# Chunk 1's q, k and x turned through DRAM instead of on TensorE, and zero matmuls in the opening, in an mLSTM with a gated FFN

## Chip, cores and metric

One NeuronCore of a Trainium2 chip runs the whole kernel. The metric is the device time of one execution in microseconds. The time before is 537.03 us, the median of three runs (535.66 to 537.51).

## What is computed

An mLSTM recurrence over 768 steps (batch 4, 8 heads, head size 40), and on its output a gated FFN. The reference, cut to what matters:

```
for t in range(S):                                   # S = 768
    m_new = max(f[t] + m, i[t])
    C = exp(f[t]+m-m_new) * C + exp(i[t]-m_new) * outer(v[t], k[t])
    n = exp(f[t]+m-m_new) * n + exp(i[t]-m_new) * k[t]
    y[t] = sigmoid(o[t]) * (C @ q[t]) / max(|n . q[t]|, 1)
x = y as (3072, 320)
out = (sigmoid(x @ w_gate) * (x @ w_val)) @ w_out    # d_ff = 1536
```

The three FFN weights come as 64-bit floats, 3.9 MB each.

## The kernel before

The 768 steps are cut into 6 chunks of 128, and a chunk into 4 units, one for each batch entry: unit n is chunk n // 4, batch entry n % 4. In a chunk the recurrence is attention with a decay matrix: scores k.q (`s`), times the decay (`t`), times v (`av`), plus what the state of earlier chunks gives (`in`), then the state's update (`cs`, `cm`, `ca`). For the scores, q and k must stand with the head's dims on the partitions; they are loaded with time on the partitions, so they must be turned. The same holds for the unit's output x, which the FFN needs turned (`xh`, `xl`: its high part and the rest).

There are three ways of turning, chosen by the chunk (lines 649 to 760). Chunk 0 (`padded`) uses TensorE transposes of zero-padded pairs of heads. Chunk 1 (`not stacked`, lines 726 to 759) makes six TensorE transposes a unit (L736), copies them out of PSUM (L745, L747), spreads q over a block-diagonal matrix by a mask product (`qb`, L752), and makes the scores of a group of heads with one fp32 matmul of 384 or 256 columns (L759; an fp32 matmul is two instructions in the trace). Its x is turned by three more transposes (L948), after a copy (`xd`, L942). Chunks 2 to 5 (`bounced`, lines 649 to 697) turn 32 x 32 blocks on VectorE (`tq`, L656), write them to a DRAM buffer `scq` with four DMAs (`tw`, L647), read q and k back stacked by six DMAs (`sr`, L668) and once more plainly for the state product (`sq`, L688, L690), form high and low parts with a sign vector on ScalarE and VectorE (`sh`, `sl`, L674, L680), and make the scores of a head with one fp32r matmul of 128 columns (L697). Their x goes the same way through `scx` (`tx`, `xw`, `xr`, L926 to L938). The stacked tiles `bh` and `bl`, the tile `kh` of the block transposes and the tile of the turned x have one buffer each; `scq` and `scx` have two, taken in turn by the batch entry.

The FFN of a chunk goes over 12 slices of d_ff. A step `n` makes two products of gate and value (`u0`, `u1` with the rests `r0`, `r1`: L1025, L1029, L1030), their activation and product (`th`, `gx`, `gh`, `gl`), and the down projection (`dn`, L1062 to L1064). In chunk 0 the weights are split into high and low parts as they come in (`wd` loads, `wa` to `wl` work on them).

All instructions are issued in the order of one list written out in the kernel, `ORDER` (lines 42 ff.); an engine runs its own in that order. Nearly every DMA is issued on SP's queue, in list order; only the input gates and q of unit 0 go on ScalarE's. Every element of the list is a function `@op(name)`. The first FFN step stands behind the attention of units 0 to 2. In the opening, `wm` (L379) runs eight fp32 matmuls on zeros; the tile of zeros is `warm`, of which `tab` (L309) overwrites one element to load the activation table.

What switches the ways, in `PARAM`: 'QT': 2 (chunks from 2 on turn q and k through DRAM), 'XT': 2 (the same for x), 'V32': 1.

Of the kernel before, what the change touches and what calls it, by code (L numbers as in the profile page):

```python
# [8 lines left out]
F32 = mybir.dt.float32  # L9
# [13 lines left out]
    'V32': 1,  # L23
    'AV': 2,
    'QT': 2,
    'XT': 2,
# [5 lines left out]
    'PAD': 1,  # L32
    'warm': 8,
    'eng': {
# [8 lines left out]
    i1 li lf i2 wdo0 i0 wz lq0 wdr0 i3 i5 ga tap pz tr0.0 cp0.0 gm0 gb war0 wdv0 tac sp0.0 wao0 wav0 sp1.0 sp1.1 gc  # L43
    wbo0 wco0 sp0.1 gm1 ee0.0 em0.0 wbr0 wcr0 woo0 who0 wor0 lv0 l10 ee1.0 em1.0 wbv0 wcv0 lk0 wlo0 ee0.1 em0.1
    tr0.1 lk1 cp0.1 gs0 lk2 tr1.1 whr0 ee1.1 wlr0 lq1 tr1.0 cp1.0 wdo4 wov0 cp1.1 gm2 whv0 ld2 lq2 wao4 s0.0 wdo1
    wao1 lq4 dl0 t0.1 wbo4 s1.0 kw0 i8 em1.1 dl1 kw1 gs1 lk3 lo0 lq3 tab cs0 cm0.0 wco4 cm0.1 tr2.1 lv1 woo4 who4
    wlv0 l11 tr2.0 t0.0 wdo3 ee2.1 lo1 og0 t1.0 ee2.0 cp2.0 cp2.1 t1.1 av0 wlo4 av1 gm3 wbo1 gm4 tr3.0 ns0 wao3 og1
    cp3.0 nd0 wdg0 ro0 ld3 xd0 xt0 xh0 gm5 ns1 nd1 wco1 wm wdg1 wag0 em2 woo1 who1 ro1 wbg0 xd1 xt1 xh1 wdr1 wbo3
    lv3 wco3 xl0 xl1 s2.0 wcg0 lo2 ee3.1 dl2 kw2 ee3.0 wlo1 em3 gd wag1 wog0 u1.0 lv2 r1.0 l12 t2.0 tbp t2.1 tbc
    whg0 wlg0 og2 wbg1 woo3 wcg1 dl3 cs1 cm1.0 cm1.1 tr3.1 cp3.1 who3 wog1 u0.0 r0.0 kw3 th0 gx0 wlo3 war1 whg1 gh0  # L50
    av2 ns2 u0.1 nd2 gl0 l13 r0.1 s3.0 wbr1 u1.1 dn0.0 wdv1 ld4 r1.1 ee4.1 wcr1 lk4 ee4.0 ro2 wor1 th1 wlg1 t3.0
    wav1 t3.1 tr4.0 gx1 wdo5 wao5 lo4 wbo5 cp4.0 whr1 wbv1 lo3 wcv1 wov1 u0.2 cs2 cm2.0 em4 gs4 wlr1 dn0.1 cm2.1
    wco5 gh1 xd2 ld5 gl1 av3 whv1 nd3 r0.2 dn1.1 og3 ns3 wlv1 xt2 dn1.0 u1.2 r1.2 ee5.0 woo5 th2 xh2 wdo2 i6 tdp xl2
    wao2 wbo2 tdc tr4.2 qb4.0 dl4 ro3 cp4.2 xd3 u0.3 who5 r0.3 gx2 gh2 qb4.2 wco2 gl2 th3 woo2 xt3 xh3 xl3 s4.0 u1.3
# [24 lines left out]
    ee8 em8 gh19 gl19 nd7 dn19.1 s8.0 th20 xh6 u1.20 dn19.0 xl6 r1.20 s8.2 cd7.1 kw7 ro7 dl8 t8.0 kw8 s8.1 gx20
    sr9.00 sr9.02 sr9.10 sr9.12 sr9.01 u0.21 r0.21 t8.2 gh20 th21 cs7 cm7.1 cm7.0 gl20 u1.21 r1.21 gx21 sr9.11 t8.1  # L80
    u0.22 dn20.1 r0.22 in8 ca7.1 gh21 gl21 dn21.1 th22 ti8 u1.22 r1.22 gx22 lk10 l18 dn20.0 gh22 ob0.2 dn21.0 va8
    vb8 u0.23 r0.23 xd7 xt7 gl22 sh9.0 da8 db8 av8.0 sl9.0 xh7 lq11 lv9 th23 av8.1 tq10 tw10.1 av8.2 ad8 u1.23 r1.23
    gx23 ns8 sh9.1 gh23 dn22.1 u0.24 r0.24 gl23 kw9 cd7.0 lv11 dn22.0 tw10.0 sl9.1 dn23.1 xl7 u1.24 r1.24 dn23.0
    tw10.3 ea10 th24 gx24 s9.1 ob0.3 nd8 u0.25 t9.1 r0.25 lq14 tw10.2 gh24 s9.2 gl24 dn24.1 u1.25 og9 r1.25 ee10
    s9.0 sq10.0 t9.2 ro8 t9.0 cs8 sr10.00 sr10.02 th25 gx25 dn24.0 in9 sr10.01 sr10.10 sr10.11 u0.26 da9 r0.26 lk11
    em10 dl10 gh25 gl25 u1.26 r1.26 sr10.12 th26 ca7.0 u0.28 cm8.0 dn25.1 dn25.0 gx26 r0.28 ti9 cm8.1 lq12 kw10 gh26
    cd8.1 gl26 u1.28 r1.28 th28 dn26.1 gx28 gh28 db9 tx8 xw8.3 sh10.0 dn26.0 gl28 sq10.1 u0.27 r0.27 dn28.3 tq11
    tw11.2 tw11.1 th27 xw8.1 tw11.0 l19 dn28.2 u1.27 lq13 r1.27 va9 l111 ca8.1 sh10.1 sl10.0 ld11 gx27 vb9 tw11.3
    u0.29 r0.29 av9.0 av9.1 av9.2 gh27 th29 sl10.1 s10.2 gl27 dn27.1 u1.29 ad9 r1.29 nd9 ns9 dn27.0 gx29 u0.30 r0.30
    t10.2 gh29 xw8.2 s10.0 s10.1 gl29 dn29.3 dn29.2 u1.30 t10.1 ro9 xw8.0 t10.0 th30 lv10 r1.30 in10 cd10.1 gx30  # L90
# [102 lines left out]
def mlstm_then_gated_ffn_kernel(  # L193
# [89 lines left out]
    @op("wz")  # L283
    def _():
        nc.vector.memset(warm, 0.0)

    if PARAM["PAD"]:
        DP = 64
        pads = []
# [826 lines left out]
```

## Time and profile before

| | |
|---|---|
| median of three runs | 537.03 us |
| profiled execution, its own time | 532.81 us |
| span of the profiled execution | 531.1 us |
| mean granted clock of TensorE | 0.986 |
| TensorE busy | 514.0 us (97%) |
| VectorE, ScalarE, GpSimd busy | 333.9, 244.1, 251.9 us |
| moved by DMA | 74.15 MB |

A profile is one execution. PE is TensorE's matmuls, PEld its weight loads, DVE VectorE, ACT ScalarE, POOL GpSimd, SPq the queue on which DMAs are issued. Records of matmuls that follow each other overlap, so their durations hold latency; the distance between starts is what one costs in a row. The DMA share is the mean busy share of 16 DMA engines and can pass 1 where packets overlap. PEclk is the granted clock of TensorE as a share of 2.4 GHz.

### The profile page before, as it was taken

Reading aid. Unit: us, or ns where it says so; the run is one execution under the profiler, and the core shown is the slowest. Engines: PE = TensorE matmul, PEld = TensorE weight load, DVE = VectorE, ACT = ScalarE, POOL = GpSimd, SP = SyncE. Lnnn points to the kernel's source line nnn. Section 1 sums busy time; section 2 is a strip of 40 time slices with the busy share of each in tenths; the row PEclk is TensorE's granted clock in tenths of the full one; section 3 lists DMA queues with packets and bytes.
Section 4 is the critical chain, followed back from the end, with each engine's and each line's share of the span. In section 5 each row is a group of like instructions: output and inputs, shape, how many; then the busy total and the mean of one; then the engine's idle time right before and its main releaser. Section 6 shows DMA issues by size and latency. Waiting matters only on the chain.

```text
span 531.1 us, 10974 instructions
## 1 busy us (share of the span) xinstructions
PE 514.0 (97%) x4005; PEld 474.4 (89%) x4005; DVE 333.9 (63%) x700; ACT 244.1 (46%) x560; POOL 251.9 (47%) x293
## 2 busy tenths in 40 slices
PE   5899999999999999999999999899999999999997
PEld 5789998889999999998888888789888888999996
DVE  6789876877667766665675555957263584643322
ACT  4768757644554353644542353342263334223222
POOL 3746465572474267467485427364513624601000
PEclk9689999999999999999999999999999999999999
DMA  8986868238678988699968699497545846201000
GB/s 190 236 216 185 215 157 225 79 91 174 133 159 162 173 178 189 140 184 179 187 117 157 136 204 158 112 173 178 147 99 94 152 98 134 56 26 42 14 14 25
DMA packets 222477, 74.15 MB, mean 140 GB/s; under 512 B 167380, under 2 KB 214168, under 8 KB 222424
## 3 DMA queue, kind: packets, MB, share of 16 engines
q1 hardware_dynamic: 221336, 73.20, 63.9%
q8 instruction: 31, 0.51, 0.4%
q10 hardware_dynamic: 1088, 0.26, 0.2%
q14 instruction: 22, 0.18, 0.1%
HBM read 61.54 MB, written 11.90 MB: 138 GB/s over the span
## 4 chain that ended last, share of the span: by engine, by line
PE 79%; DMA 7%; SPq 4%; ACT 3%; DVE 3%; issue 2%; POOL 2%; DVEq 0%; POOLq 0%; ACTq 0%
PE pg L1025 33%; PE po L1062 7%; PE po L1064 6%; PE po L1063 6%; PE pg L1029 5%; PE pg L1030 5%; PE av L893 3%; PE av L886 3%; PE s L697 2%; PE cs L969 2%; PE in L869 2%; DMA scx<-tx 2%; DMA qs<-scq 2%; SPq L647 2%; PE s L759 1%
## 5 line engine op out<-in xcount | busy, mean ns | idle before, releaser
L1042 DVE SCALAR_TENSOR_TENSOR pg<-sg,pg 128x256 f32<-128x256 f32 (+1 forms) x103 | 54.8, 532 | 98.1 <-PE pg L1030 72.4
L1047 ACT ACTIVATE gh<-pg 128x256 fp32r<-128x256 f32 (+1 forms) x103 | 48.2, 468 | 139.7 <-DVE pg L1042 122.5
L1025 PE MATMUL pg<-xh,wh 128*128 128x256 f32 (+1 forms) x412 | 105.8, 338 | 0.3 <-ACT xh L955 0.2
L1025 PE MATMUL pg<-xh,wl 128*128 128x256 f32 (+1 forms) x412 | 101.2, 327 | 0.0
L1025 PE MATMUL pg<-xl,wh 128*128 128x256 f32 (+1 forms) x412 | 100.9, 326 | 0.0
L1062 PE MATMUL po<-oh,gh 128*128 128x320 f32 x288 | 94.3, 327 | 0.3 <-ACT gh L1047 0.3
L1064 PE MATMUL po<-oh,gl 128*128 128x320 f32 x288 | 89.4, 310 | 0.2 <-DVE gl L1052 0.2
L1063 PE MATMUL po<-ol,gh 128*128 128x320 f32 x288 | 88.9, 309 | 0.0
L1035 ACT ACTIVATE sg<-pg 128x256 f32<-128x256 f32 (+1 forms) x103 | 48.0, 466 | 66.0 <-PE pg L1030 61.0
L1025 PEld LDWEIGHTS pg<-xl,wh 128*128 128x128 f32 x412 | 69.1, 190 | 7.5 <-POOL xl L959 0.6
L1025 PEld LDWEIGHTS pg<-xh,wl 128*128 128x128 f32 x412 | 69.0, 189 | 7.2
L1052 DVE TENSOR_TENSOR gl<-pg,gh 128x256 fp32r<-128x256 f32 (+1 forms) x103 | 54.1, 526 | 33.0 <-ACT gh L1047 31.7
L1025 PEld LDWEIGHTS pg<-xh,wh 128*128 128x128 f32 x412 | 67.1, 189 | 3.8 <-DVE gl L1052 0.8
L1029 PE MATMUL pg<-xh,w 128*128 128x256 f32 (+1 forms) x206 | 68.3, 331 | 0.0
L1030 PE MATMUL pg<-xl,w 128*128 128x256 f32 (+1 forms) x206 | 67.1, 326 | 0.0
L1062 PEld LDWEIGHTS po<-oh,gh 128*128 128x128 f32 x288 | 54.4, 189 | 3.9 <-ACT gh L1047 0.6
L1063 PEld LDWEIGHTS po<-ol,gh 128*128 128x128 f32 x288 | 54.3, 189 | 3.3
L842 POOL TENSOR_TENSOR dr<-d 128x1024 f32<-128x1024 f32 x16 | 30.3, 1894 | 52.8 <-DVE d L823 50.6
L1064 PEld LDWEIGHTS po<-oh,gl 128*128 128x128 f32 x288 | 54.1, 188 | 1.1 <-DVE gl L1052 1.0
L638 POOL TENSOR_SCALAR_AFFINE_SELECT d<-d 128x1024 f32<-128x1024 f32 x22 | 26.2, 1190 | 41.0 <-ACT d L634 34.9
L823 DVE TENSOR_TENSOR d<-s,d 128x384 f32<-128x384 f32 (+2 forms) x68 | 34.9, 526 | 12.7 <-PE s L697 7.3
L630 POOL TENSOR_TENSOR d<-at,d 128x1024 f32<-128x1024 f32 x16 | 31.3, 1959 | 22.5 <-DMA d<-mscr 18.8
(156 smaller groups left out, 911.3 us busy)
## 6 DMA issues: line engine op xcount, KB each, us to landing
d<-mscr SPq DMA_DIRECT2D x22, 512.0 KB
ks<-scq SPq DMA_DIRECT2D x48, 168.0 KB
qs<-scq SPq DMA_DIRECT2D x48, 168.0 KB
scq<-tq SPq DMA_DIRECT2D x64, 80.0 KB
su_o<-in_moe_w_out_dram SPq DMA_DIRECT2D x12, 320.0 KB
v<-in_v_dram SPq DMA_DIRECT2D x24, 160.0 KB
o<-in_o_gate_dram SPq DMA_DIRECT2D x24, 160.0 KB
out_dram<-ob SPq DMA_DIRECT2D x24, 160.0 KB
```

The source lines that it names most:

```text
L630: E("ea", n).tensor_tensor(dm[n], a, dm[n], ALU.subtract)
L823: nc.vector.tensor_tensor(y, ps_[n, g][:, :nh, :], y, ALU.mult)
L1025: nc.tensor.matmul(p, w[y][:, a, fs], x[c][:, a, n0:n1], start=(i + a == 0), stop=False)
L1029: nc.tensor.matmul(pg[n, y], w2[y][:, fs], xh[c][:, 2, n0:n1], start=False, stop=False)
L1030: nc.tensor.matmul(pg[n, y], w2[y][:, fs], xl[c][:, 2, n0:n1], start=False, stop=True)
L1035: nc.scalar.activation(s, pg[n, 0], AF.Tanh, scale=0.5)
L1042: nc.vector.scalar_tensor_tensor(sgs[n], gate, 1.0, pg[n, 1], ALU.add, ALU.mult)
L1047: nc.scalar.activation(ghs[n][:, :nt], sgs[n], AF.Copy)
L1052: E("gl", n).tensor_tensor(gls[n][:, :nt], sgs[n], ghs[n][:, :nt].bitcast(F32), ALU.subtract)
L1062: nc.tensor.matmul(p, ghs[n][:, ts], oh[:, j, :], start=(j == 0), stop=False)
L1063: nc.tensor.matmul(p, ghs[n][:, ts], ol[:, j, :], start=False, stop=False)
L1064: nc.tensor.matmul(p, gls[n][:, ts], oh[:, j, :], start=False, stop=(j == NF - 1))
```

## The change

'QT' and 'XT' become 1: the units of chunk 1 (4 to 7) go the way of the later chunks. With that, for these four units, `tr`, `cp`, `qb`, `xd` and `xt` leave the list, and `tq`, `tw`, `sr`, `sh`, `sl`, `sq`, `tx`, `xw` and `xr` enter it. 'V32' becomes 0. Fourteen functions `wk0` to `wk13` are added, each one bf16 matmul of 512 columns on the zeros of `warm`, into PSUM tile `po3`. `ORDER` is written anew over its whole length. A branch `paired` is added for scores in pairs of heads; with 'RT': 0 no unit takes it.

```
-    'V32': 1,
+    'V32': 0,
...
-    'QT': 2,
-    'XT': 2,
+    'QT': 1,
+    'XT': 1,
...
+    'RT': 0,
     'warm': 8,
+    'NW': 14,
...
+    for x in range(PARAM["NW"]):
+        @op(f"wk{x}")
+        def _(x=x):
+            pw = pst("po3", [P, NT], f"pwarm{x}")
+            zeros = warm.bitcast(BF16)
+            nc.tensor.matmul(pw, zeros[:, :P], zeros[:, :NT], start=True, stop=True)
...
+        paired = bounced and c < PARAM["RT"]
...
-        for g, (h0, nh) in enumerate(((0, 4), (1, 4)) if padded else GROUPS):
+        for g, (h0, nh) in enumerate(((0, 4), (1, 4)) if padded or paired else GROUPS):
```

The start of the new list, and the order in which TensorE's work stands in it up to the first FFN steps (from the list):

```
+    i1 lf wz pz wdr0 i0 i3 tab wk7 wk0 i5 wk12 i2 li ga wk8 gm0 lk0 sp0.0 wdo3 lq0 tap gb war0 wbr0 lv0 tr0.0 wao3
...
wk7 wk0 wk12 wk8 sp0.0 tap tr0.0 sp1.0 sp0.1 tr0.1 sp1.1 tr1.0 s0.0 wk13 tr2.0 wk11 wk9 tr1.1 av0 cs0 tr2.1 s1.0
wk5 s2.0 av1 wk3 wk4 wk6 wk2 cs1 xt0 wm tr3.0 wk10 xt1 tr3.1 u0.0 r0.0 u1.0 r1.0 av2 wk1 u0.1 r0.1 s3.0 u0.2 r0.2
```

Before, that order was:

```
tap tr0.0 sp0.0 sp1.0 sp1.1 sp0.1 tr0.1 tr1.1 tr1.0 s0.0 s1.0 cs0 tr2.1 tr2.0 av0 av1 tr3.0 xt0 wm xt1 s2.0 u1.0 r1.0
```

SP's queue around unit 5's way through DRAM, in the new list (`wd`: weight slices; `l`: loads; `ld`: decay rows):

```
tw5.1 tw5.3 tw5.2 tw5.0 ld5 lk6 wdg3 sq4.0 wdg4 sq4.1 ld6 sq5.0 wdv4 lv5 wdo6 tw6.2 sr5.00 lo5 sr5.10 sr5.01 sr5.02
sr5.12 sr5.11 tw6.1 lk7 tw6.3 wdr4 wdo7 lq7 sq5.1 wdg5 lv6 tw6.0 wdo8 ld7 sr6.00
```

## Rows read from the trace of the kernel before

**Rows 1.** The page: the head, TensorE's busy time, and three rows over 40 equal slices of the span (granted clock in tenths, DMA share in tenths).
```profile
span 531.1 us, 10974 instructions
PE 514.0 (97%) x4005; PEld 474.4 (89%) x4005; DVE 333.9 (63%) x700; ACT 244.1 (46%) x560; POOL 251.9 (47%) x293
...
PEclk9689999999999999999999999999999999999999
DMA  8986868238678988699968699497545846201000
```

**Rows 2.** The waits of TensorE, longest first: us in total, times, longest us.
```profile
PE tat L423 <- DVE gin L385: 4.7, 1, 4.7
PE av L886 <- DVE t L874: 1.4, 1, 1.4
```

**Rows 3.** The timeline of TensorE in chunk 1's attention: start us, us, engine, line, operation, output <- inputs, shapes, count.
```profile
112.69 0.27 PE L736 MATMUL pt<-ident,q 128*120 128x128 f32 x1
...
113.06 0.31 PE L1063 MATMUL po<-ol,gh 128*128 128x320 f32 x1
113.20 0.31 PE L1064 MATMUL po<-oh,gl 128*128 128x320 f32 x1
113.35 0.81 PE L759 MATMUL s<-qbd,qkt 120*128 120x384 f32 x2
...
114.14 0.31 PE L1063 MATMUL po<-ol,gh 128*128 128x320 f32 x1
...
116.90 0.49 PE L948 MATMUL xt<-ident,x 128*128 128x128 f32 x3
117.22 0.27 PE L736 MATMUL pt<-ident,q 128*80 128x128 f32 x1
```

**Rows 4.** The same timeline at the scores of a unit of chunk 2. Between the two rows stands one record of L1062.
```profile
181.94 0.78 PE L697 MATMUL s<-qs,ks 126*128 126x128 f32 x6
...
182.76 0.31 PE L1063 MATMUL po<-ol,gh 128*128 128x320 f32 x1
```

**Rows 5.** Windows of the opening: from:to in us, their length, busy time of PE, PEld, DVE, ACT, POOL (with instructions), granted clock, DMA share, GB/s.
```profile
16.00:17.00 1.00, 0.19 (x2) 0.19 (x4) 0.90 (x3) 1.00 (x3) 0.93 (x2) 1.00 1.11 346
17.00:18.00 1.00, 1.00 (x16) 0.81 (x15) 0.47 (x2) 0.66 (x2) 0.92 (x3) 0.86 1.18 243
18.00:19.00 1.00, 1.00 (x7) 0.97 (x5) 0.93 (x3) 0.59 (x2) 0.85 (x3) 0.50 1.13 199
...
30.00:31.00 1.00, 1.00 (x6) 1.00 (x6) 0.96 (x3) 0.96 (x3) 0.00 (x0) 0.50 0.00 0
31.00:32.00 1.00, 1.00 (x9) 1.00 (x9) 0.93 (x4) 0.47 (x2) 0.74 (x3) 0.82 0.03 8
...
17.80:31.20 13.40, 13.04 (x63) 12.17 (x61) 9.51 (x28) 7.95 (x24) 5.12 (x9) 0.50 0.78 207
```

**Rows 6.** The timeline of TensorE: its first FFN matmul, and two starts of pairs of 512-column matmuls later on.
```profile
35.21 0.50 PE L1025 MATMUL pg<-xh,wh 128*128 128x256 f32 x2
...
71.29 0.62 PE L1025 MATMUL pg<-xh,wh 128*128 128x512 f32 x2
71.75 0.62 PE L1025 MATMUL pg<-xh,wl 128*128 128x512 f32 x2
```

**Rows 7.** The DMAs of the way through DRAM, over the whole span (16 units): output <- input, queue, operation, count, KB each.
```profile
ks<-scq SPq DMA_DIRECT2D x48, 168.0 KB
qs<-scq SPq DMA_DIRECT2D x48, 168.0 KB
scq<-tq SPq DMA_DIRECT2D x64, 80.0 KB
...
scx<-tx SPq DMA_DIRECT2D x64, 40.0 KB
xf<-scx SPq DMA_DIRECT2D x16, 128.0 KB
qk<-scq SPq DMA_DIRECT2D x16, 120.0 KB
xf<-scx SPq DMA_DIRECT2D x32, 32.0 KB
...
qk<-scq SPq DMA_DIRECT2D x16, 40.0 KB
```

**Rows 8.** Windows of longer stretches; columns as in rows 5.
```profile
45.00:117.00 72.00, 70.60 (x447) 63.11 (x448) 55.94 (x127) 46.90 (x124) 43.41 (x59) 1.00 0.62 163
117.00:200.00 83.00, 83.00 (x760) 81.41 (x759) 59.02 (x130) 39.94 (x93) 41.95 (x52) 1.00 0.78 159
170.00:270.00 100.00, 99.63 (x907) 94.79 (x906) 65.92 (x142) 49.07 (x111) 61.22 (x69) 1.00 0.89 176
...
2.00:11.00 9.00, 5.65 (x26) 5.26 (x27) 6.98 (x22) 4.01 (x9) 3.09 (x9) 1.00 1.08 246
...
100.00:120.00 20.00, 20.00 (x114) 17.42 (x113) 14.77 (x33) 11.21 (x28) 11.10 (x14) 1.00 0.27 75
```

**Rows 9.** Groups by line of the work that a unit turned through DRAM puts on VectorE and ScalarE: shapes, count | busy us, mean ns of one | idle time before.
```profile
L680 DVE SCALAR_TENSOR_TENSOR qs<-qs,rsign,qt 126x1024 fp32r<-126x1024 f32 x16 | 21.5, 1346 | 4.8 <-ACT qt L674 3.3 <-DMA scx<-tx 1.3
...
L656 DVE STREAM_TRANSPOSE tq<-q 128x320 f32<-128x320 f32 x16 | 8.0, 501 | 1.7 <-DMA scq<-tq 1.7
...
L674 ACT ACTIVATE qt<-qs,rsign 126x1024 fp32r<-126x1024 f32 x16 | 18.4, 1150 | 14.8 <-DMA qs<-scq 8.2 <-DMA scq<-tq 4.6 <-issue 1.4
```

More of the change, by code (lines that the diff above doesn't have):

```diff
@@ L647, in _, with paired_scores @@
                     nc.sync.dma_start(dv[:, :, ts], src()[ts].rearrange("j (n i) -> j n i", i=32))
+        def paired_scores():
+            @op(f"s{n}.0")
+            def _():
+                for x in range(2):
+                    ps_[n, x] = pst(P_(f"s{n}.{x}"), [P, 4, L], f"s_{n}_{x}")
+                for y in range(4):
+                    for x in range(2):
+                        rs = slice(DP * x, DP * x + D)
+                        nc.tensor.matmul(ps_[n, x][:, y, :], sop[n][rs, 1, y, :], sop[n][rs, 0, y, :], start=True, stop=True)
         if bounced:
@@ L658, in unit @@
             turned_out("tw", sc[: 2 * DM], lambda: split[n].rearrange("p x d -> p (x d)"))
-            for x, y in ((1, "k"), (0, "q")):
-                for i in range(3):
-                    @op(f"sr{n}.{x}{i}")
-                    def _(x=x, y=y, i=i):
-                        if (n, x) not in stk:
-                            stk[n, x] = sbt("bl" if x == 0 else "bh", [P, 9, L], F32R, f"{y}s_{n}")[:, :H]
-                        src = sc[x * DM : x * DM + DM].rearrange("(h d) t -> d h t", d=D)
-                        src = bass.AP(tensor=src.tensor, offset=src.offset, ap=[[src.ap[0][0], DX]] + [list(z) for z in src.ap[1:]])
-                        nc.sync.dma_start(stk[n, x][i * DX : (i + 1) * DX].bitcast(F32), src)
-                @op(f"sh{n}.{x}")
-                def _(x=x, y=y):
-                    r = 3 * DX
-                    sgn[n, x] = t = sbt("st", [P, H, L], F32, f"{y}t_{n}", 3)
-                    nc.scalar.activation(t[:r].bitcast(F32R), stk[n, x][:r].bitcast(F32), AF.Copy, scale=rsign[:r, 5 - x : 6 - x])
-                @op(f"sl{n}.{x}")
-                def _(x=x):
-                    r = 3 * DX
-                    R = stk[n, x]
-                    nc.vector.scalar_tensor_tensor(R[:r], R[:r].bitcast(F32), rsign[:r, 3 - x : 4 - x], sgn[n, x][:r], ALU.mult, ALU.add)
@@ new lines, in unit, with _ @@
+            if paired:
+                for x in (1, 0):
+                    for e in range(2):
+                        @op(f"sr{n}.{x}{e}")
+                        def _(x=x, e=e):
+                            if n not in sop:
+                                sop[n] = sbt(f"b{'hl'[b % 2]}", [P, 2, 4, L], F32, f"qkt_{n}")
+                            src = sc[x * DM : x * DM + DM].rearrange("(y e d) t -> d e y t", e=2, d=D)
+                            nc.sync.dma_start(sop[n][DP * e : DP * e + D, x], src[:, e])
+            else:
+                for x, y in ((1, "k"), (0, "q")):
+                    for i in range(3):
+                        @op(f"sr{n}.{x}{i}")
+                        def _(x=x, y=y, i=i):
+                            if (n, x) not in stk:
+                                stk[n, x] = sbt("bl" if x == 0 else "bh", [P, 9, L], F32R, f"{y}s_{n}")[:, :H]
+                            src = sc[x * DM : x * DM + DM].rearrange("(h d) t -> d h t", d=D)
+                            src = bass.AP(tensor=src.tensor, offset=src.offset, ap=[[src.ap[0][0], DX]] + [list(z) for z in src.ap[1:]])
+                            nc.sync.dma_start(stk[n, x][i * DX : (i + 1) * DX].bitcast(F32), src)
+                    @op(f"sh{n}.{x}")
+                    def _(x=x, y=y):
+                        r = 3 * DX
+                        sgn[n, x] = t = sbt("st", [P, H, L], F32, f"{y}t_{n}", 3)
+                        nc.scalar.activation(t[:r].bitcast(F32R), stk[n, x][:r].bitcast(F32), AF.Copy, scale=rsign[:r, 5 - x : 6 - x])
+                    @op(f"sl{n}.{x}")
+                    def _(x=x):
+                        r = 3 * DX
+                        R = stk[n, x]
+                        nc.vector.scalar_tensor_tensor(R[:r], R[:r].bitcast(F32), rsign[:r, 3 - x : 4 - x], sgn[n, x][:r], ALU.mult, ALU.add)
@@ L690, in _ @@
                         nc.sync.dma_start(qk[n][: 2 * D, 2], sc[2 * r : DM])
-            for g, (h0, nh) in enumerate(GROUPS):
-                @op(f"s{n}.{g}")
-                def _(g=g, h0=h0, nh=nh):
-                    ps_[n, g] = p = pst("pa", [P, 3, L], f"s_{n}_{g}")
-                    for m in range(nh):
-                        nc.tensor.matmul(p[:, m, :], stk[n, 1][: 3 * DX, h0 + m, :], stk[n, 0][: 3 * DX, h0 + m, :], start=True, stop=True)
+            if paired:
+                paired_scores()
+            else:
+                for g, (h0, nh) in enumerate(GROUPS):
+                    @op(f"s{n}.{g}")
+                    def _(g=g, h0=h0, nh=nh):
+                        ps_[n, g] = p = pst("pa", [P, 3, L], f"s_{n}_{g}")
+                        for m in range(nh):
+                            nc.tensor.matmul(p[:, m, :], stk[n, 1][: 3 * DX, h0 + m, :], stk[n, 0][: 3 * DX, h0 + m, :], start=True, stop=True)
         elif padded:
@@ L716, in _ @@
                         nc.vector.tensor_copy(sop[n][:, x], pt_[n, x])
-            @op(f"s{n}.0")
-            def _():
-                for x in range(2):
-                    ps_[n, x] = pst(P_(f"s{n}.{x}"), [P, 4, L], f"s_{n}_{x}")
-                for y in range(4):
-                    for x in range(2):
-                        rs = slice(DP * x, DP * x + D)
-                        nc.tensor.matmul(ps_[n, x][:, y, :], sop[n][rs, 1, y, :], sop[n][rs, 0, y, :], start=True, stop=True)
+            paired_scores()
         elif not stacked:
```

288 lines of the change are left out of this document (146 added, 142 removed).

## The prediction

> **What bounds the kernel now.** I read the page first: TensorE is busy for 514.0 of 531.1 us, no other engine comes near, and the clock row is full except in the opening [rows 1]. So the span is TensorE's work plus 17 us in which it has none. The waits of TensorE say where those lie: the longest is the 4.7 us before its first instruction, and the next is 1.4 us [rows 2]; no later wait is worth removing by itself. A microsecond of TensorE work taken out after the opening is therefore worth a microsecond of span, unless something else becomes late. The second thing to see is the clock: it falls to half between 17 and 19 us, after a stretch in which TensorE had little to do, and returns only between 31 and 32 us [rows 5]. The third is the DMA engines, which are fully busy from 2 to 11 us (1.08) but only 0.62 in the stretch from 45 to 117 us, where chunk 1 is worked on [rows 8].
>
> **TensorE work of chunk 1.** The four units 4 to 7 lose six q/k transposes, three score matmuls and three x transposes each. Matmul records overlap, so I cost by what follows. One record of a down-projection matmul follows the next after 0.14 us. A pair of transposes at 112.69 and one such matmul end by 113.06: 0.23 us for the pair, 0.69 for three. A score matmul of 384 columns at 113.35, and one such matmul, end by 114.14: 0.65 us; two of these and one of 256 columns (two thirds, 0.43) make 1.73. Three x transposes run from 116.90 to 117.22: 0.32 [rows 3]. Sum 2.74 us for a unit. In their place come eight fp32r matmuls of 128 columns: six of them at 181.94 and one down-projection matmul end by 182.76, so 0.113 us each and 0.91 for a unit [rows 4]. Net 1.83 us, and 7.3 us for four units. All of it lies after 45 us, at full clock and with TensorE busy throughout: on the path. **Term: -7.3 us.**
>
> **The opening.** Fourteen bf16 matmuls of 512 columns on zeros are added; the eight older fp32 ones stay. No row has a bf16 matmul that wide. The nearest are 512-column fp32r ones, two in 0.46 us, so 0.23 us each at full clock and an estimated 0.46 at half [rows 6]. Four stand before the first score of the gates is spread, where TensorE now waits 4.7 us: hidden by that wait, and if the wait were gone they would cost 0.9. They do wait for the activation table, since the table's warm-up writes one element of the zeros; so does the load of the input gates, which now stands behind it on ScalarE's queue. VectorE's first scan waited for GpSimd's mask, which is now built earlier; I price this at nothing, at most 1 us. The other ten are on the path: 2.3 us at full clock, 4.6 at half. What they can win is the stretch at half clock: 13.4 us in which TensorE was busy 13.04 [rows 5], 6.7 us at full clock. Bounds: -6.7 + 2.3 = -4.4, and +4.6 if nothing is won. Three of the ten stand right behind the unit-0 scores and the first transposes of unit 2, where the gaps lay that came before the fall; that speaks for the lower end. Against it: from 18 to 31 us TensorE was busy nearly all the time and yet stayed at half clock, so being busy did not by itself bring it back. **Term: -2 us**, nearer to the lower end, bounds -4.4 to +4.6. The Trainium skill, "TensorE: Matmul & The Clock Gate" (section Part 1, What's actually happening), says that the throttled state is the default and that activity releases it; taken alone this would give the term -4.4 and a total 2.4 us lower. The rows of the slow stretch, busy and at half clock, agree with it only in part.
>
> **The DMA queue.** Each of the four units now sends its turned q and k out (4 x 80 KB), its turned x (4 x 40), and reads them back (6 x 168, 120 + 40, 128 + 2 x 32): 1840 KB and 19 more issues on SP's one queue [rows 7]. Four units: 7.5 MB, 76 issues. In the 100 us from 170 on, with the same mix of traffic, a share of 0.89 moved 176 GB/s, so a full share moves 198, and 7.5 MB take 38 us of all sixteen engines. The DMA work of 45 to 200 us was 0.62 x 72 + 0.78 x 83 = 109 us [rows 8]. With 38 it is 147.5 us, and TensorE, 7.3 us shorter, wants to be through in 155 - 7.3 = 147.7. The queue would have to run at a share of 1.0 for 150 us. Shares of 1.08 are there while the queue is full (2 to 11 us), 0.89 is the highest over 100 us, in a stretch that asked for no more [rows 8]. In the new list the bounce stands between weight slices: each read-back waits for four write-outs, reads into buffers that the scores of the unit before still hold, and behind the waiting read stand weight slices and loads of later units. Bounds: 0 at a share of 1.0, +18 at 0.89. I take 0.97, 152 us: **term +5 us**, since the list puts other transfers between most write-outs and their reads.
>
> **At nothing.** VectorE gains two transposes of 0.5 us, two sign combines of 1.3 and the x transpose a unit [rows 9], some 4.2 us, and loses copies and a mask product; against 56 of 72 and 59 of 83 us busy [rows 8] its 17 us fit, but to 0.9 of the stretch: at most 2 us. ScalarE's 2.3 us a unit fit in its room. GpSimd loses mask products. The flag V32 and the new paired branch change nothing, as no unit takes that branch.
>
> **Sum.** -7.3 - 2 + 5 = -4.3 us. The profiled execution took 532.81 us, its span 531.1; it lies 4.2 us below the median of 537.03, so I set the difference against the median: **532.7 us**. Differences within 0.3% (1.6 us) can't be told from none.
>
> **Rivals.** (a) Everything arrives in time: the share stays near 1.0, the clock holds. -7.3 - 4.4 = -11.7, so 525.3 us. For it: shares over 1 while the queue is full. Against: no 100 us at such a share. (b) The transfers of chunk 1 become the bound, and it is slower. If the share is 0.89, TensorE stands 18 us, before the scores of units 5 and 6 and before the first FFN steps of chunk 1: -7.3 - 2 + 18 = +8.7, so 545.7 us. It decides from 9.3 us of such waits on, a share under 0.94. For it: the 0.89, and the short distance in the list between x's way out and the first FFN step that needs it. Against: DMA was only 0.27 busy from 100 to 120 us [rows 8], so there was room exactly there. The Trainium skill, "VectorE: DVE Perf Modes" (section Rules for kernel authors), advises TensorE for a 128 x 128 transpose, which speaks for this rival; the net 1.83 us of TensorE per unit, bought with 9.5 us of DMA, is what the rows make of it. (c) The opening wins nothing: the half-speed stretch stays and the ten matmuls cost 4.6. -7.3 + 4.6 + 5 = +2.3; with the clock half won it is about zero: 537 us.
>
> **Chances.** Forecast 0.36, (a) 0.24, (b) 0.27, (c) 0.13. Faster by over 0.3%: the forecast and (a), 0.60. Within: (c), 0.13. Slower: (b), 0.27. The range takes in (a) and most of (b): 524 to 544 us; the forecast's own is 528 to 536.
>
> **What would show it.** TensorE busy near 505 us and no transposes from chunk 1. In the clock row, a short or missing dip in the opening, and the first FFN matmul before the 35.2 us of now [rows 6]. In the windows from 45 to 200 us, a DMA share of 0.95 or more. Waits of TensorE should be a few us more there, ending in scores of units 5 to 7 or in xh of chunk 1. I am wrong if the share stays under 0.9 and TensorE still never waits (then (a)), or if waits over 9 us stand there (then (b)).

## The result, and the profile after

The kernel after takes 540.64 us (median of 20 runs) against 536.28 us for the kernel before: ratio 1.0082 with a 95% interval of 1.0056 to 1.0109. One of the 20 runs took 1246.89 us at a full clock; the ratio leaves it out. The kernel is slower by 4.4 us, where 4.3 us less was forecast. The time lies inside the range and on rival (b)'s side of it, though not at its 545.7; what came is a change the other way.

The two profiled executions lie further apart than the medians: 543.91 us after (span 542.2) against 532.81 before (span 531.1), 11.1 us. The profile of after lies 3.3 us above its median, that of before 3.5 below its own. So the rows below show where time goes, and the ratios how much.

The head of the page of after, answering to [rows 1]: span, TensorE, the clock row and the DMA row over 40 slices.

```profile
span 542.2 us, 11086 instructions
PE 516.1 (95%) x3991; PEld 473.9 (87%) x3991; DVE 348.3 (64%) x708; ACT 249.6 (46%) x560; POOL 246.7 (45%) x285
...
PEclk9979899998999879999999999999999999999999
DMA  8989999898997976978988598895366663521000
```

The clock row of before had one dip, at slices 2 and 3; this one has a dip at slice 3, and new ones at slices 5, 10, 14 and 15. TensorE's idle time rose from 17.1 to 26.1 us. Its waits, answering to [rows 2] (us in total, times, longest us), say where:

```profile
PE pg L1055 <- DVE gl L1082: 7.9, 5, 3.3
PE pg L1055 <- ACT sg L1065: 5.4, 4, 2.5
PE pwarm L392 <- ACT warm L315: 2.3, 1, 2.3
PE cs L999 <- DVE d L853: 1.7, 2, 1.5
```

The first two did not exist before. A `pg` matmul is the first half of an FFN step; it waits until its buffer has been read by the SwiGLU of an earlier step, on ScalarE (`sg`) and VectorE (`gl`). The windows, answering to [rows 8] (from:to, length, busy time of PE, PEld, DVE, ACT, POOL, clock, DMA share, GB/s), with the opening first:

```profile
0.00:45.00 45.00, 39.27 (x284) 33.06 (x284) 35.95 (x93) 30.62 (x87) 23.48 (x44) 0.92 0.92 227
45.00:117.00 72.00, 66.28 (x415) 59.49 (x414) 58.48 (x129) 50.81 (x123) 36.02 (x46) 0.98 0.99 220
117.00:200.00 83.00, 73.78 (x592) 70.26 (x592) 53.17 (x112) 33.22 (x77) 44.59 (x52) 0.92 0.90 174
```

From 45 to 200 us the DMA share is 0.99 and 0.90 (0.62 and 0.78 before), and TensorE stands idle for 5.7 + 9.2 = 14.9 us, against 1.4 + 0 before. The clock has fallen too, to 0.98 and 0.92 where it was 1.00. The timeline of ScalarE and TensorE around two of the waits, in order of time (start us, us, engine, line, operation; in brackets the idle time before it and what ended it):

```profile
62.20 0.43 ACT L505 ACTIVATE dc_r<-su_r 128x256 f32<-128x256 f32 x1 [3.46 <-DMA su_r<-in_moe_w_val_dram]
62.54 0.37 ACT L1065 ACTIVATE sg<-pg 128x256 f32<-128x256 f32 x1
...
62.96 0.50 PE L1055 MATMUL pg<-xh,wh 128*128 128x256 f32 x2 [2.49 <-ACT sg L1065]
...
123.33 0.52 ACT L985 ACTIVATE xh<-xf 128x384 fp32r<-128x384 f32 x1 [4.15 <-DMA xf<-scx]
123.76 0.47 ACT L505 ACTIVATE dc_o<-su_o 128x320 f32<-128x320 f32 x1
124.14 0.58 ACT L1077 ACTIVATE gh<-pg 128x512 fp32r<-128x512 f32 x1
...
125.77 1.22 PE L1055 MATMUL pg<-xh,wh 128*128 128x512 f32 x2 [3.31 <-DVE gl L1082]
```

Read them as a queue. TensorE waits for `sg`, a 0.37 us operation that had its input long before; ScalarE stood for 3.46 us at the entry ahead of it, which waited for a weight slice. At 126 us the entry ahead is `xh` of unit 4: 4.15 us for x to come back from DRAM, the change's own transfer, and `gh` behind it starts late, and with it `gl` on VectorE. At 166 and 186 us (1.76 and 2.29 us) it is the sign work on the turned q and k of chunk 2. So the late transfer is not one kind: weight slices, chunk 1's x and chunk 2's q and k are all late. All go through SP's one queue to one pool of DMA engines. SP's timeline shows when the two transfers above were issued (start us, us):

```profile
57.07 0.58 SPq L496 DMA_DIRECT2D su_r<-in_moe_w_val_dram  x1
117.92 1.28 SPq L968 DMA_DIRECT2D xf<-scx  x1
```

The issue of the weight slice ended at 57.7 us, 1.1 us before ScalarE came to read it, and the slice was in use 4.5 us after that end; another one of its size that ScalarE waited for (at 90 us) was in use after 2.6. Unit 4's x took 4.1 us (1.8 for unit 5's), and the q and k at 166 and 186 us 6.1 to 6.3, where those that ScalarE waited for in before took 3.3 to 5.8. So all four were long on their way, and the slice was also issued so shortly before its reader that 2.6 us would have left a wait. SP's queue may be a second brake: from 45 to 200 us the records of DMA issues on its timeline cover 126 of the 155 us, against 73 in before. How much each does, the sixteen engines and SP's queue, no run below separates: each that adds or removes bytes adds or removes issues with them.

What each wait costs besides itself stands in these stretches, windows as above. Each begins where TensorE is at work again or soon after:

```profile
62.96:67.30 4.34, 4.34 (x21) 4.34 (x22) 3.46 (x7) 3.85 (x8) 1.32 (x1) 0.61 1.02 158
125.80:129.20 3.40, 3.40 (x9) 2.73 (x10) 1.57 (x4) 1.51 (x2) 2.22 (x5) 0.56 1.12 187
186.60:197.40 10.80, 9.62 (x45) 9.25 (x44) 6.49 (x8) 1.00 (x3) 5.17 (x4) 0.53 0.75 158
```

TensorE is busy, at a granted clock of 0.61, 0.56 and 0.53, that is mostly at the lower of its two levels (1.2 GHz), after waits of 2.49, 3.31 and 2.29 us. 0.39 x 4.34 + 0.44 x 3.40 + 0.47 x 10.80 = 8.3 us are lost there, on top of the 14.9 us of waits. After the wait of 1.76 us at 166 us the clock stayed full (1.00 from 166.5 to 180 us).

### The profile page after: what moved, and what is told of

It is laid out like the page before. It is cut to its first block, busy times and chain, and to the rows that moved or that the text cites. A ratio compares the mean times of both kernels' runs of the same rounds, so it can differ in the third digit from the quotient of the medians.

```text
span 542.2 us, 11086 instructions
## 1 busy us (share of the span) xinstructions
PE 516.1 (95%) x3991; PEld 473.9 (87%) x3991; DVE 348.3 (64%) x708; ACT 249.6 (46%) x560; POOL 246.7 (45%) x285
## 4 chain that ended last, share of the span: by engine, by line
PE 70%; DMA 10%; SPq 6%; ACT 5%; DVE 3%; issue 3%; POOL 1%; DVEq 0%; ACTq 0%; POOLq 0%
PE pg L1055 29%; PE po L1092 6%; PE po L1093 6%; PE po L1094 6%; PE pg L1059 5%; PE pg L1060 5%; PE av L916 3%; PE s L734 3%; DMA qs<-scq 2%; SPq L661 2%; PE in L899 2%; SPq L702 2%; PE cs L999 2%; DMA su_r<-in_moe_w_val_dram 1%; DMA xf<-scx 1%
## 5 line engine op out<-in xcount | busy, mean ns | idle before, releaser
L1092 PE MATMUL po<-oh,gh 128*128 128x320 f32 x288 | 92.9, 323 | 0.0
L1093 PE MATMUL po<-ol,gh 128*128 128x320 f32 x288 | 90.3, 313 | 0.0
L1093 PEld LDWEIGHTS po<-ol,gh 128*128 128x128 f32 x288 | 55.4, 192 | 3.0
L1092 PEld LDWEIGHTS po<-oh,gh 128*128 128x128 f32 x288 | 55.5, 193 | 2.9
L1094 PEld LDWEIGHTS po<-oh,gl 128*128 128x128 f32 x288 | 55.3, 192 | 0.9 <-DVE gl L1082 0.9
L989 POOL TENSOR_TENSOR xl<-xf,xh 128x384 fp32r<-128x384 f32 x20 | 20.5, 1030 | 62.7 <-ACT xh L985 56.4
```

The source lines that it names most:

```text
L1092: nc.tensor.matmul(p, ghs[n][:, ts], oh[:, j, :], start=(j == 0), stop=False)
L1093: nc.tensor.matmul(p, ghs[n][:, ts], ol[:, j, :], start=False, stop=False)
L1094: nc.tensor.matmul(p, gls[n][:, ts], oh[:, j, :], start=False, stop=(j == NF - 1))
```

## The experiments

A ratio is to runs of the kernel before that were taken together with the run. "Idle" is 155 us less TensorE's busy time from 45 to 200 us in the profile, "lost to the clock" the mean of span x (1 - granted clock) over the runs. Before has 1.4 us idle and, over five sets of runs, 7.0 to 7.6 us lost; after has 14.9 and 12.3. Waits, idle time and clock by stretch come from one profiled execution each.

**1. Without the matmuls on zeros** (after).

```diff
 ORDER (after):
-    wk7 wk0 wk12 wk8 wk13 wk11 wk9 wk5 wk3 wk4 wk6 wk2 wk10 wk1
```

> The changed kernel without its fourteen zero matmuls, all else as it is. If they hold the clock up in the opening, the stretch at half clock comes back to some 13 us (7 us in the changed kernel) and the kernel is about 3 us slower than the changed one, 544 against a before of 536. If they only cost their own time, it is 2 us faster, 538.5. If all that happens in the opening is caught up by the waits for transfers later, the time stays within 1 us of 540.6.

Measured: 537.49 us, ratio 1.0066 [1.0035, 1.0096]. That is 0.16% under after, inside both intervals: the matmuls bring nothing that can be measured in the time. In the opening they cost. In the five profiles of the new list without them (runs 1, 10, 12, 13, 14) the first FFN matmul starts at 33.2 to 34.2 us; in the seven with them (after and runs 2, 3, 4, 6, 9, 11) at 33.8 to 36.9, two microseconds later on average; before has it at 35.2. The clock from 0 to 45 us is 0.85 to 0.92 without them and 0.81 to 0.96 with them (0.85 before): in the new list they do not hold it.

**2 to 4. The old ways of turning, in the new list.**

```diff
 e2:  -    'XT': 1,     +    'XT': 2,
      -    tx4 xw4.* xr4.*      +    xd4 xt4      (units 4 to 7; xh, xl move up behind them)
 e3:  -    'QT': 1, 'V32': 0,   +    'QT': 2, 'V32': 1,
      -    tq4 tw4.* sr4.* sh4.* sl4.* sq4.*    +    tr4.* cp4.* qb4.*      (units 4 to 7)
 e4:  both
```

> The changed kernel, but with chunk 1's x turned on TensorE as before (q and k still through DRAM, same list elsewhere). Queue theory (the DMA engines are the bound from 45 to 200 us): 9 us of the 38 us of added transfers go, 1.3 us of TensorE work come back; TensorE's waits there fall from 15 to about 8 us and the time to about 535. Chain theory (the serial way out of and into the chip for a unit, not the load on the engines, makes TensorE wait): only the waits for xh of chunk 1 go, the ones before scores stay; 538 to 540.

> The changed kernel, but with chunk 1's q and k turned on TensorE as before (x still through DRAM, same list elsewhere). Queue theory: 29 of the 38 us of added transfers go, the DMA share from 45 to 200 us falls to about 0.8, TensorE's waits there to under 3 us and the clock no longer falls; TensorE has 6 us more to do: 533 to 536. List theory (the new order is bad whatever way the units take): still 540 or more, with the waits in the same places.

> The new list and the zero matmuls, with all of chunk 1 turned on TensorE as before. Queue theory: no waits over 1 us between 45 and 200 us, 7.3 us more TensorE work than the changed kernel, the opening as in the changed kernel: 532 to 536, not slower than before. List theory: 540 to 548, as the 7.3 us of work come back and the waits stay.

Measured: x back on TensorE 538.15 us, 1.0061 [1.0027, 1.0095]; q and k back 541.17, 1.0104 [1.0051, 1.0156]; both back 541.29, 1.0107 [1.0057, 1.0157]. By their own expectations run 2 came out as chain theory has it (538 to 540), runs 3 and 4 as list theory has it (540 or more, 540 to 548); queue theory, 532 to 536, is met by none. Windows of the last:

```profile
45.00:117.00 72.00, 66.28 (x417) 58.01 (x416) 52.05 (x120) 44.96 (x120) 37.92 (x51) 1.00 0.54 150
117.00:200.00 83.00, 77.00 (x639) 72.60 (x638) 56.91 (x119) 35.03 (x85) 46.60 (x55) 1.00 0.73 148
```

Undoing the change's way of turning does not give the time back. The DMA share is 0.54 and 0.73, below that of before, and yet 11.7 us are idle, in waits of at most 1.8 us behind many releasers. So a kernel with the new list can be as slow without chunk 1's transfers. The entries for the old ways were placed by me, after no tuning, and in runs 2 and 4 `xh` and `xl` moved as well, by up to 140 places, so this does not show what of the 11.7 us is the new list and what my placing. With this placing the way through DRAM is no measurable loss inside the list: 1.0082 with it, 1.0107 without, intervals overlapping.

**5. The matmuls on zeros in the old list.**

```diff
 ORDER (before):
+    wk7 wk0 wk12 wk8 (behind wz)   wk13 (s0.0)   wk11 wk9 (tr2.0)
+    wk5 wk3 (av0)   wk4 wk6 wk2 (av1)   wk10 (wm)   wk1 (u0.0)
```

> The kernel before with the fourteen zero matmuls put into its own list: four ahead of its first work, the others behind the scores of unit 0, ahead of and between the products of units 0 and 1, and around the older zero matmuls. If they keep the clock up, the half-clock stretch of 13.4 us shrinks by about half and the time falls by 1 to 4 us (532 to 535). If not, it rises by 2 to 4 us.

Measured: 538.61 us, 1.0041 [1.0011, 1.0071]. Windows of the opening, and the row in front of the first FFN matmul:

```profile
18.00:20.00 2.00, 2.00 (x16) 1.78 (x13) 1.93 (x5) 0.27 (x2) 1.85 (x4) 0.50 1.12 198
20.00:22.00 2.00, 1.64 (x10) 1.24 (x9) 1.40 (x3) 1.69 (x8) 1.37 (x3) 0.50 1.00 223
22.00:24.00 2.00, 1.52 (x10) 1.33 (x10) 1.93 (x6) 2.00 (x8) 0.75 (x1) 0.65 1.10 284
24.00:26.00 2.00, 1.94 (x17) 1.59 (x16) 0.58 (x3) 1.71 (x5) 1.09 (x1) 1.00 0.33 119
```
```profile
33.53 1.53 PE L734 MATMUL s<-qkt 40*128 40x128 f32 x16 [1.68 <-DVE xl L968]
34.98 0.50 PE L1034 MATMUL pg<-xh,wh 128*128 128x256 f32 x2
```

The zeros do what they could be meant for: the clock is back at 24 us instead of between 31 and 32 [rows 5], and the runs lose 3.2 us to it instead of 7.6. But the first FFN matmul comes at 34.98 instead of 35.21 us [rows 6], because the scores in front of it now wait 1.68 us for `xl` on VectorE. In this profile the opening's end was set by another engine, and TensorE's speed there was worth 0.2 us. The 2.2 us that the kernel loses lie later: from 45 to 200 us 3.9 us are idle instead of 1.4. No row settles why.

**6 and 8. Fewer bytes, in after and in before.** The later weight slices are taken from a constant tile instead of being loaded, 7.9 MB less; all other instructions stay.

```diff
+        const_src = (i >= 4) if part == 3 else (i >= 2)
             if const_src: return bmask[:, 0, :64]... (in place of the staging tile)
-                nc.sync.dma_start(st, ...)      (none where const_src)
```

> The changed kernel, leaving out the loads of the later weight slices (four of six of gate, value and rest, eight of twelve of the output weights, 7.9 MB); their splitting works on a constant tile instead, so the output is not the reference's. Queue theory: with as many bytes taken off the queue between 45 and 120 us as the change put on it, TensorE's waits from 45 to 200 us fall from 15 us to under 4, no fall of the clock there, 525 to 530. Chain theory: the way of a unit through DRAM is as long as before, the waits before scores and xh stay, 538 to 541.

> The kernel before with the same 7.9 MB of weight loads left out as in the sixth run (the later weight slices come from a constant tile, so the output is not the reference's). Theory A, the 7.5 MB of chunk 1 overfilled the DMA engines: the kernel before had room there (its DMA share was 0.62 from 45 to 117 us), so taking bytes away gives it little: ratio to before 0.993 to 1.003. Rival B, any kernel of this family gains from fewer weight bytes, and the 10.6 us of the sixth run say nothing of the change: ratio 0.975 to 0.985. Share from 45 to 117 us near 0.4 by both.

Measured: after with fewer bytes 530.69 us, 0.9885 [0.9839, 0.9931]; before with fewer bytes 532.94, 0.9961 [0.9938, 0.9985]. Windows of the first, then of the second:

```profile
45.00:117.00 72.00, 70.72 (x458) 64.51 (x457) 64.58 (x145) 54.63 (x135) 40.21 (x51) 1.00 0.79 146
117.00:200.00 83.00, 76.93 (x699) 74.65 (x698) 57.64 (x119) 37.88 (x88) 45.91 (x53) 0.98 0.90 175
```
```profile
45.00:117.00 72.00, 71.92 (x457) 64.42 (x457) 57.83 (x131) 47.39 (x127) 44.36 (x59) 1.00 0.28 61
117.00:200.00 83.00, 82.95 (x754) 80.67 (x753) 57.92 (x129) 38.91 (x92) 41.63 (x51) 1.00 0.76 156
```

The same relief is worth 1.97% in after (10.6 us) and 0.39% in before (2.1 us). That is the clearest result of the study: after pays 8.5 us more than before for bytes that both load, about 3 us either way by the three intervals. With fewer bytes the changed kernel is faster than before with as few, 0.9885 against 0.9961. That its price is one of crowding fits, and is argued: the cut takes 24 issues off SP's queue as well as bytes off the engines, it takes away the very weight slice that ScalarE stood for at 63 us, and the new list with the old ways and fewer bytes was not run. In the first, the waits at 63 and 126 us are gone and 7.4 us remain idle (under 4 were expected), mostly from 117 us on, where the share is still 0.90. In the second the share from 45 to 117 us is 0.28, where 0.4 was expected.

**7. The bytes alone.** Before, with 72 transfers of chunk 1's 7.5 MB on SP's queue, issued from 43 to 172 us; nobody reads them. One more transfer, at the start, fills the scratch. The writes come from a constant tile and add as many packets under 512 bytes as the change does (16.5 thousand). The reads do not match it: they go from DRAM to DRAM in 512 packets over 8 KB, where the change adds 10.9 thousand of 512 bytes to 2 KB.

```diff
 ORDER (before):
+    dw0.0 ... dw0.9 dr0.0 ... dr0.7 (four times, from dn2.1 to s9.1)
```

> The kernel before with 72 more DMAs from 50 to 150 us on SP's queue, as many packets of 128 and of 512 bytes as the change adds (7.5 MB), into DRAM buffers that nobody reads; nothing waits for them. Queue theory: loads, weights and chunk 2's ways come late behind them; TensorE waits 8 to 15 us more and the kernel is 6 to 15 us slower, 542 to 551. Chain theory: the engines have room, less than 3 us slower.

Measured: 553.68 us, 1.0300 [1.0249, 1.0350]. Its windows:

```profile
45.00:117.00 72.00, 66.70 (x419) 58.83 (x417) 51.23 (x118) 43.59 (x116) 39.62 (x54) 1.00 0.77 199
117.00:200.00 83.00, 77.00 (x633) 74.29 (x632) 52.94 (x116) 34.15 (x79) 35.91 (x48) 0.96 0.86 184
```

In the old list these bytes cost 16 us, more than the change's own, and the share was only 0.77 and 0.86: TensorE was idle 11.3 us with the engines well under full on average. So the share of a long window says little of what transfers will cost. Here too SP's queue is loaded: its issues cover 112 of the 155 us.

**9. Work in the waits** (after).

```diff
+    zk0 (before u0.6)   zk1 (before u1.15)   zk2 (before u1.27), each:
+        for _n in range(16):
+            nc.tensor.matmul(pw, fill[:, :P], fill, start=True, stop=True)      # bf16, 256 columns
```

> The kernel after, with 16 bf16 matmuls of 256 columns, whose result nobody reads, in front of each of three FFN steps that TensorE waited for (2.5 us at 63 us, 3.3 at 126, 2.3 at 186). Theory C, a wait costs twice, once as idle time and once because TensorE's clock stands at half after it: the three dips (1.7 + 1.7 + 5 us lost in the profiled execution) go or shrink, the clock from 45 to 200 us is 0.98 or more, and the ratio to before falls from 1.008 to 0.998 or less. Rival D, the clock's dips follow something else than the waits, or new waits take their place: the clock stays near 0.975 and the ratio at 1.008 to 1.012, since the matmuls cost up to 5 us where no wait hides them.

Measured: 538.39 us, 1.0052 [1.0023, 1.0082]. Its windows:

```profile
45.00:117.00 72.00, 67.40 (x438) 59.86 (x437) 57.43 (x130) 51.19 (x127) 34.06 (x45) 1.00 1.03 224
117.00:200.00 83.00, 77.45 (x647) 72.98 (x647) 56.53 (x118) 35.26 (x82) 48.90 (x55) 0.98 0.91 178
```

The dips go: 1.00 and 0.98 instead of 0.98 and 0.92, and 7.9 us lost per run instead of 12.3. So the clock falls because of the waits, as theory C has it, and work in them holds it from 45 to 200 us. The Trainium skill, "TensorE: Matmul & The Clock Gate" (section Part 1, What's actually happening), has the clock released by activity; these rows agree. But of the 4.4 us only 1.6 (0.30%) show in the ratio, against the 1% that C expected, and 0.30% lies inside the intervals. A reason that fits, and is not shown: when TensorE runs faster between two waits it arrives earlier at the next one, and the data it waits for does not come sooner.

**10. x on TensorE and no zeros** (edits of 1 and 2 together).

> The kernel after with x of chunk 1 transposed on TensorE and without the fourteen matmuls on zeros; q and k still go through DRAM. Both parts alone measured 1.0061 and 1.0066. If the two add up (each about 1 us under the kernel after): ratio to before 1.003 to 1.005. If the new list itself is what costs, as theory L has it: 1.005 or more. If q and k through DRAM pay for themselves once the queue has room (theory A): 1.000 or less.

Measured: 536.31 us, 1.0001 [0.9968, 1.0035]: not to be told from before. The parts added up would have made 1.0045, just outside the interval, but that sum has the noise of three ratios; 1.000 is the edge of what theory A expected, so q and k through DRAM may pay for themselves here, but the interval does not settle it. Its waits stand at 54 to 63 us (5.5 us), with a clock of 0.95 from 45 to 117 us.

**11, 12 and 14. The late readers moved back** (of after, of run 10, and of run 11 without the zeros). The lists of 11 and 14 move eleven entries, that of 12 nine.

```diff
 ORDER:
-    wdr2 war2 dn3.1 ...                   +    ... gx5 gh5 war2 wbr2
-    tq5 u1.4 ...                          +    ... gl4 tq5
-    sh9.0 cd8.1 gl22 ... sh9.1 r1.23      +    ... gh23 sh9.0 sh9.1 ... r0.24 sl9.0
-    sh10.1 dn26.1 th28 sl10.1 ... sh10.0  +    ... gh28 sh10.1 sh10.0 gl28 sl10.1
-    xh4 sr7.11 u1.14 xl4 (not in 12)      +    ... gh14 xh4 th15 tw8.0 gl14 xl4
```

> The kernel after, same instructions and bytes, with ten entries of the order list moved back by 5 to 45 places: the sign work on the turned q and k of units 9 and 10, xh and xl of unit 4, the first two steps of one residual weight slice and the turn of unit 5, all of which stood in ScalarE's or VectorE's queue ahead of a SwiGLU step and waited there for a transfer. Theory E, the loss is late transfers times the place of their first reader in an in-order queue: the waits of 2.5, 3.3, 1.8 and 2.3 us at 63, 126, 166 and 186 us go, the clock's dips behind them too; of the 9.9 us of waits and 8.5 us of clock half comes back: ratio to before 0.990 to 1.000. Rival F, the DMA engines are simply short of time, so the same data is needed a few us later all the same: new waits stand behind the old places, ratio 1.004 to 1.010.

> The tenth run (x of chunk 1 on TensorE, no matmuls on zeros; ratio 1.0001) with the same entries moved, but for those of unit 4's x. Its waits stand at 54 to 63 us (5.5 us together, with the clock at half behind them for some 7 us) and at 185 us (1.6). Theory E: most of these go, ratio 0.988 to 0.996, which beats the kernel before. Rival F: 0.998 to 1.003.

> The eleventh run (ten entries moved; ratio 1.0046) without the fourteen matmuls on zeros. In the list of after leaving them out gave 0.16% (1.0066 against 1.0082). If the opening is not bounded by TensorE, so that the matmuls bring nothing and cost what no wait hides: ratio 1.001 to 1.004. If they hold the clock: 1.005 or more.

Measured: 536.12 us, 1.0046 [1.0017, 1.0076]; 536.89 us, 1.0048 [1.0018, 1.0079]; 536.75 us, 1.0062 [1.0031, 1.0094]. Waits of run 11 over the whole span, then its windows:

```profile
PE po L1094 <- DVE gl L1082: 2.9, 4, 2.1
PE pg L1055 <- ACT sg L1065: 2.7, 4, 0.9
PE pwarm L392 <- ACT warm L315: 2.3, 1, 2.3
PE pg L1055 <- DVE gl L1082: 2.2, 4, 1.1
PE cs L999 <- ACT qkt L751: 2.1, 1, 2.1
PE s L734 <- DMA v<-in_v_dram: 2.0, 1, 2.0
```
```profile
45.00:117.00 72.00, 66.44 (x421) 58.32 (x420) 57.76 (x131) 51.45 (x125) 34.44 (x46) 1.00 1.02 222
117.00:200.00 83.00, 77.19 (x642) 73.57 (x641) 55.23 (x119) 35.85 (x82) 49.76 (x54) 0.98 0.94 180
```

All four waits left their places, and with them the dips: 9.2 us lost to the clock per run instead of 12.3. But 11.4 us are still idle, in many waits of up to 2.1 us behind the old places, and the DMA share rose to 1.02 and 0.94. So rival F holds by the ratio, and theory E only in part: here the place of a late transfer's reader decided how the wait was divided (and by that what the clock lost), and moved little of its sum. Moving entries won nothing for run 10 (1.0048 against 1.0001, intervals overlapping); that misses both of run 12's forecasts. Leaving out the zeros won nothing in the moved list: 1.0062 is in the range expected for zeros that hold the clock, but it can't be told from run 11's 1.0046, and the runs lose 9.8 us to the clock against 9.2.

**13. Run 10 with work in its one long wait** (the sixteen matmuls of run 9 before u0.6).

> The tenth run (x of chunk 1 on TensorE, no matmuls on zeros; ratio 1.0001 [0.9968, 1.0035]) with 16 bf16 matmuls of 256 columns, whose result nobody reads, in front of the FFN step that TensorE waits for at 63 us (2.7 us, and the clock at half behind it, 3.6 us lost from 45 to 117 us). Theory C, the clock is lost by that wait: the clock from 45 to 117 us is 1.00 instead of 0.95, ratio 0.993 to 0.998, which would beat both kernels. Rival D: what the clock gives back is eaten by the matmuls and by the next wait: 0.999 to 1.004.

Measured: 533.43 us against 534.59, ratio 0.9989 [0.9962, 1.0016]. Its windows:

```profile
45.00:117.00 72.00, 66.85 (x428) 58.98 (x427) 56.78 (x127) 51.03 (x125) 35.03 (x48) 1.00 1.01 222
117.00:200.00 83.00, 79.16 (x721) 76.81 (x722) 61.52 (x125) 39.65 (x91) 45.52 (x54) 1.00 0.89 169
```

The clock is held (1.00 in both; 7.1 us lost per run, as much as before loses), and this is the best of the new list's kernels: 0.9% under after. The clock does what theory C expected and the ratio falls to the edge of rival D's range. It cannot be told from before, so it does not beat both. Against run 10 the gain lies inside the intervals, so neither this run nor run 9 measures the price of the clock alone.

## Why the prediction was wrong

- **What bounds the kernel** was read rightly: TensorE's work sets the time, and a microsecond of idle time is a microsecond of span, unless the clock falls too. That last clause was missing.
- **TensorE work, -7.3 us.** The 24 transposes of q and k and half of x's are gone from the page; scores on `qs`, `ks` went from 128 to 160. Busy time rose by 2.1 us; taking off 14 x 0.23 = 3.2 for the zeros and the clock's loss while busy, some 8.3 in the new dips less the 3.1 that the opening gained (45 x 0.15 before, 45 x 0.08 now), leaves -6.3: near the term, by an estimate from one profile that takes the zeros at the forecast's price.
- **The opening, -2 us.** Measured about 0: the first FFN matmul moved from 35.21 to 34.72 us in the profile of after, and leaving the zeros out changes nothing measurable in the time. The zeros won nothing and cost about the 2.3 us that the forecast had priced them at: without them the new list reaches the first FFN matmul two microseconds earlier (run 1). What shortened the opening was the new order. In the old list the zeros did raise the clock, and VectorE's `xl` then ended the opening (run 5); the forecast had not asked which engine ends it.
- **The DMA queue, +5 us.** This is the step that failed: late transfers were priced as a shortfall of the average share. The share of 0.97 made 5 us (147.5 / 0.97 less 147.7 is in fact 4.4). From 45 to 200 us the share was 0.94 on average, for which the same formula gives 9.2 us, and the waits were 13.5 us more than before in the profile. Run 7 shows the error apart from the change: 11.3 us idle at 0.77 and 0.86. In both, one late transfer stopped an engine that works its list in order, with the work TensorE needed queued behind it. The engine time came out near the forecast, 0.99 x 72 + 0.90 x 83 = 146.0 us against 147.5, but partly by luck: from 45 to 200 us it moved 5.4 MB more than before (220 x 72 + 174 x 83 against 163 x 72 + 159 x 83), not 7.5, so a byte cost more engine time than the row from 170 us on had given.
- **The new order** of the whole list stood in no term, without a reason. Run 4 keeps it, takes chunk 1's transfers out and still has 11.7 us idle.
- **At nothing.** VectorE had the time for the added work, as said (58.5 of 72 and 53.2 of 83 us busy), and ScalarE too (50.8 and 33.2); what they did not have was the order. The text looked for the wait "before the scores of units 5 and 6" and in xh. xh of unit 4 is the longest wait, but it reaches TensorE through `gh` and `gl`, not through the FFN step that reads x.
- **The clock** stood in no term, though the rows of the opening showed what a stretch of little work does to it. Per run 12.3 us are lost to it against 7.0 to 7.6, some 5 us, the size of the whole slowdown. How much of that is time is open: run 9 regains 4.4 of these and 1.6 us of time, which lies inside the intervals. Over 19 runs of after, 0.01 of mean clock (5.4 us of loss) goes with 2.4 us of time, so an estimate from these two is about half.
- **Rival (b)** is nearest to what came: waits behind late transfers. It asked for 9.3 us of them and got 13.5, on readers that it did not name. "A share under 0.94" was no good mark for it: the share was 0.99 in the first stretch. The chance, 0.27, was too low, in part because the 0.27 share from 100 to 120 us [rows 8] was taken as room; in after it is 0.91 there. That chunk 1's transfers are the bound is not shown: runs 3 and 4, without them, are no faster.
- **Open:** how much of the slowdown is the transfers and how much the new list as such. Runs 6 and 8 speak for the transfers, 8.5 us. Runs 3 and 4 speak for the list, 1.04 and 1.07% slower than before with most or all of the old ways and a DMA share of 0.54 to 0.83, but their placing is mine. A list for the old kernel with chunk 1's q, k and x through DRAM was not tried, nor a run that loads SP's queue without the engines.

The Trainium skill, "VectorE: DVE Perf Modes" (section Rules for kernel authors), with its advice of TensorE for a 128 x 128 transpose, is not decided for x by these runs: run 2 is 0.2% under after, inside the intervals; runs 10 and 13 with it are the best of the new list, run 12 with it is not.

## What to carry to other kernels

When transfers are added to a kernel whose order is written by hand, don't price them by the mean DMA share alone: take the stretch, add as many bytes in packets of the same sizes to the kernel before, with nobody reading them, and see what they cost (16 us here for 7.5 MB, with larger packets for the reads). Then test the reverse in the changed kernel by taking other bytes away; the difference to the same cut in the kernel before is what the changed kernel pays more for its bytes (8.5 us). Test the rewritten list as a change of its own. Where TensorE waits for a short operation, read the queue of the engine that runs it: in the waits read here the culprit stood ahead of it in that queue. Then read SP's timeline, to see whether the transfer moved slowly or was issued late.

A wait of TensorE should be entered with the clock that follows it. And before paying for the clock in an opening, look at which engine ends the opening.

## What the runs showed of the hardware that was not expected

- After waits of 2.29 to 3.31 us TensorE ran at the lower clock for 3.4 to 10.8 us although it was busy again; the longest of these stretches has a second wait of 1.18 us in it. Sixteen matmuls in such a wait kept the clock at 1.00 (0.95 without them, runs 13 and 10).
- The sixteen DMA engines held a share of 0.99 to 1.03 for 72 us (runs 1, 9 and 11 and after), at 216 to 224 GB/s, with packets mostly under 512 bytes.
- The clock of a run goes with its time, loosely: over 19 runs of after the run at a mean granted clock of 0.964 took 545.2 us, the three at 0.987 took 537.7 to 540.6 (2.4 us for 0.01, correlation -0.70).
